# A tuned attention and feed-forward kernel on one core: 122 of some 1180 program steps put in another order

## The chip, the cores and the metric

The kernel runs on one core of a Trainium2 chip. The metric is the device time of one execution in microseconds (us); the runs shown give a median, a lowest and a highest value. A profile is one further execution, recorded by the hardware profiler: each engine's instructions with their start and duration. Engines: PE is TensorE (matmuls; PEld its weight loads), DVE is VectorE, ACT is ScalarE, POOL is GpSimd, SP is SyncE, which issues most of the transfers.

## The reference

Two blocks follow each other. The first is attention with a polynomial sketch instead of a softmax: each row of q and k (4 batches, 4 heads, 1088 rows, 32 columns) is turned into 64 features, products of two sketches of 8 values. The second is a feed-forward block with a product in place of an activation.

```python
def phi(x):
    a = np.einsum('rd,bhsd->bhsr', S1, x)
    b = np.einsum('rd,bhsd->bhsr', S2, x)
    return np.einsum('bhsi,bhsj->bhsij', a, b).reshape(*x.shape[:-1], r * r)
q_p, k_p = (phi(q), phi(k))
kv = np.einsum('bhsf,bhsd->bhfd', k_p, v)
z = np.sum(k_p, axis=2)
num = np.einsum('bhsf,bhfd->bhsd', q_p, kv)
den = np.einsum('bhsf,bhf->bhs', q_p, z)[..., None] + 1e-06
...
x = np.ascontiguousarray(attn_out.transpose(0, 2, 1, 3)).reshape(B * S, H * D)
a = x @ w1
b = x @ w2
h = a * b @ w3
return (h @ w_out)
```

x has 4352 rows of 128; w1 and w2 are 128 x 1024, w3 is 1024 x 1024 and w_out 1024 x 128.

## The kernel before

`make_steps` defines about 1180 small functions, the steps, each under a name such as `k0.gram0`, and each issues one or a few instructions. A long string, `ORDER`, names every step once. The kernel function takes the names in that order, runs each step, and then chains the instructions of every engine: an instruction of PE, DVE, ACT, POOL or SP may not be issued before the one that `ORDER` put ahead of it on the same engine. So `ORDER` alone decides what stands behind what on each engine; what one engine needs of another is waited for by semaphores. Two further tables go with it. `SLOTS` says, for each group of buffers, which buffer the first, second, third and so on allocation of the group takes. `POOL`, `ACTS` and `CPV` name the steps that run on another engine than the usual one. The large loads on SP are held back so that no more than `UNDER_WAY` of them are under way.

The steps that the prediction speaks of, with their lines before (the changed kernel has them one line up or three lines down):

- `warm0` to `warm11` (L255): fillers, matmuls of zeros that no one reads; the list `WARM` says how many each step issues (27, 2, 3, 4, 4, 4, 1, 2, 1, 1, 2, 2).
- `s.T`, `s.P` (L341, L391 to L393), `s.R` (L355): small matmuls on the sketch matrices S1 and S2; `s.c` (L369) copies the result of `s.R`, `s.blk` and `s.blkh` (L360, L365) make the block matrices from it, `s.AR` (L382) a third one.
- For each batch b of k: `kb.gram0` to `kb.gram4` (L659), the Gram matrix of k in tiny matmuls of 32 columns; `kb.lead0`, `kb.rest0` (L214, L651) split k into a leading word and the rest for it; `kb.T0`, `kb.T1` (L883, L889 to L891) and `kb.N0`, `kb.N1` (L912) bring the Gram matrix into sketch form, with `kb.Ta` and `kb.Tb` on DVE (L898, L201, L204, and L904) between them; `kb.kv0` to `kb.kv3` (L769) multiply features and v, where `kb.kp0` (L677) makes the features.
- For q: `q0.A0` (L1038), `q0.C0` (L1030) make the sketches, `qn.pt0`, `qn.pt1` (L1228, L1246) transpose the features `ph`, `qn.pc0`, `qn.pc1` (L1234) copy them out of PSUM, and `q0.x0`, `q0.x1` (L1267), `q1.x` (L1297) multiply them with k's sums.
- Of the feed-forward block: `g0.0a` to `g0.7a` (L1799) and `g0.0b` to `g0.7b` (L1809) are products of 128 rows of w1 or w2 with 512 columns of x, each one matmul in the program and two in the trace; `w1.a0` and the like (L470) prepare the weights on POOL.

A matmul on 4-byte numbers is one instruction in the code and appears as two weight loads and two matmuls in the trace (a transpose as one of each).

```python
for name in ORDER.split():
    n = len(traced)
    steps.pop(name)()
    ...
for ins in traced[seen:]:
    if ins.engine in chained:
        if ins.engine in last:
            tc.add_manual_dep(ins, last[ins.engine].name, behind, reason="order")
        last[ins.engine] = ins
```

Of the kernel before, what the change touches and what calls it, by code (L numbers as in the profile page):

```python
# [76 lines left out]
k0.load1 s.words kr0.load k0.tr1 s.pair s.low s.lead s.sum k0.max0 k0.max1 warm1 q0.max k0.tr0 warm2 kr0.tr kr0.kT  # L77
warm3 s.rest w1.load s.T s.P s.tc warm4 q0.l2 k0.kT1 s.Pc s.R k0.g k0.lead0 s.c s.blk k0.rest0 q1.tr k0.gram0 s.blkh
k1.zero s.Pm warm5 q0.l1 q0.A0 warm6 kr0.ab k0.lead1 q0.rm q0.sma q0.sta warm7 k0.kT0 v0.load v0.loadr k1.load k0.ab1
q0.sha k0.rest1 q0.C0 k0.gram1 k0.gram2 k0.gram3 k0.gram4 k0.ab0 k0.abc1 q1.max q0.C0t q0.sla q1.l2 k1.loadr s.Pp  # L80
k0.Gm k0.Gt k0.Ga w1.c1 k0.Gb k0.abc0 k0.T0 q1.l1 warm8 kr0.abc k0.kp1 q0.sca w1.j1 k0.Ta k0.kp0 k0.Gc w1.c0 k1.tr0
kr1.load k2.zero k1.tr1 k1.kT1 kr0.kp warm9 k0.N0 warm10 k0.Na warm11 k0.T1 k0.kv0 k0.Tc k0.Tb k0.N1 k0.Nb k0.Nh q1.rm
q0.al k0.Nf q0.phi0 q0.phi1 q0.A1 q0.smy w1.m1 k1.max q0.sty q0.shy k0.kv3 k0.kv1 k0.kv2 q0.sly s.KS k0.kvr kr1.tr
k0.kvm w1.m0 kr1.kT q0.p01 q1.C0 q1.C1 q0.C1 k0.kzt k2.loadr q0.pt0 q0.C1t q0.scy q0.p2 k0.kz q0.pt1 k0.kvc kr1.ab
k0.kqt q0.p12 q0.dn q0.de q0.rc w1.j0 q0.pc0 q0.pc1 q0.x0 k1.kT0 q0.x1 q0.xs0 q0.xs1 q0.xt0 w1.a0 q1.A0 k2.load
w0.load k1.lead0 q0.xc0 q0.xc1 k0.kq w1.a1 k2.max q0.xt1 k1.ab q0.xT0 q0.xT1 g0.4a q1.load g0.5a q1.sm w0.m1 q1.st
q1.Ct g0.4c g0.4b q1.sh q1.sl k1.rest0 g0.7b w0.c1 g0.7a k1.abt w0.j1 k1.gram0 w0.c0 s.RC q1.scy k1.gram1 kh2.load
q1.sca q2.tr g0.5c q1.al q1.p01 q1.p2 k1.gram2 k1.gram3 kr1.abc k1.gram4 w6.load w0.m0 g0.6b w0.j0 g0.7c g0.7m k1.Gm
q1.p12 k1.Gc g0.0a w2.load w0.a1 q1.dn q1.de q1.rc q1.bs k1.Gt g0.3a k1.Ga k1.T0 k2.kT1 k1.Gb g0.3c q1.restT g0.2a
q1.phi k1.T1 q1.pt0 g0.4m w0.a0 q2.max q2.l2 g0.6a k1.Ta k2.lead0 k2.rest0 g0.1a g0.2c k1.Tc g0.5b q3.tr g0.5m k1.Tb  # L90
# [5 lines left out]
k1.kv1 k2.T0 k1.kvr q3.sl q2.p2 k2.T1 q2.p12 q2.dn q2.de g1.4a q2.rc k3.max g0.3b g0.0m g1.1b kh3.load g1.4c k2.Ta
g1.2b q3.sc g1.2c w5.c k2.Tc k1.kvc k1.kqt k1.kq g0.3m q3.p01 g1.6c g1.3a g1.5m g1.3b q2.bs q2.phi0 q2.pT0 g1.2m g1.3c
q2.x q2.load k2.N0 k2.Tb k3.lead0 w9.a1 k2.N1 g1.4b q3.al q3.p2 q3.p12 q2.xT0 g2.5a k3.kT1 g2.5c g2.6a q3.dn q3.de
k2.Na g1.3m g2.4a g2.3a w5.m g2.4b g2.6c k3.rest0 g1.0b k2.Nr q3.rc g1.1m g1.4m g1.6b k2.Nb g0.2b kr1.kp w6.j q4.tr
g2.4c g1.6m w7.load w7.c q3.bs q4.max q2.restT w6.m w5.j w2.j q4.l2 w3.load w9.a0 k3.gram0 k3.gram1 k3.gram2 q3.load  # L100
# [5 lines left out]
w4.m g3.6c q3.restT q6.tr g3.6b g3.6m q4.Ct q4.sm w10.load f0.m k2.kp0 f4.o g3.1b f0.o g3.1m qr.max q6.max k3.kp1
q4.st k2.kv0 w4.a1 k3.kp0 k2.kv3 k2.kv1 k2.kv2 k2.kvr q4.sh qr.l2 k3.kv0 k3.kv1 f3.t k2.kvc k3.kv3 k3.kv2 k3.Na w4.a0
qr.l1 qr.rm q4.sl q4.sc q4.al k3.kvr k3.kvc g3.4a q6.l2 g3.4c g3.4b q4.p01 k3.Nr g3.3b q6.l1 w8.c g3.5a k3.Nb g2.4o
g3.4m f1.t f3.m w10.c k3.kqt g3.5c w8.m g3.3m q4.p2 q6.rm k3.kq f1.m f1.o q6.A0 q6.C0 w10.j q6.C1 g3.1o f3.o w8.j
q4.p12 q6.At g3.2b w10.m q6.Ct q4.dn g3.7a q6.sm q6.st w8.a0 w10.a0 qr.A0 qr.C0 qr.C1 g3.0o g2.1o g3.7c w10.a1 g0.3o  # L110
# [1824 lines left out]
```

## Time and profile before

| what | value |
|---|---|
| median of 3 runs | 245.37 us (245.28 to 245.43) |
| the profiled execution's own span, first to last instruction | 244.1 us |
| PE busy | 236.2 us (97% of the span), 2724 matmuls |
| DVE busy | 206.7 us (85%) |
| POOL busy | 161.9 us (66%) |
| ACT busy | 123.5 us (51%) |
| DMA packets | 31935, 22.06 MB |
| mean granted clock of TensorE | 0.998 of full speed |

The span does not hold what lies around the program, so it is 1.27 us shorter than the median of the runs. A line of the page or of a view names the engine, the line of the code, the operation and the tiles (out<-in, with the shape). "Idle" or "wait" is time in which an engine ran nothing, and the name behind it is what it seems to have waited for; "issue" means that nothing in the profile explains it. A window gives, for each engine, the busy time and the number of instructions in a stretch, then the granted clock, the share of the DMA engines in use and the GB/s.

### The profile page before, as it was taken

To read this page: it belongs to the slowest core of one execution; us is meant where nothing else is said; L and a number is where in the kernel's file an instruction comes from. 1 tells how busy PE (TensorE), PEld (TensorE's weight loads), DVE (VectorE), ACT (ScalarE), POOL (GpSimd) and SP (SyncE) were. 2 spreads that over 40 slices of the span, in tenths; PEclk is the share of its full clock that TensorE was granted. 3 is DMA by queue.
4 is the path that set the end of the run, shared out by engine and by line. 5 is a ranking of instruction groups with operands and counts; after the bars stand their busy time and mean duration, and the time that the engine had idled before them with its cause. 6 is when DMAs were issued, how large, how long until landed. Compare 5 with 4: busy or idle time off the path is not lost.

```text
span 244.1 us, 6745 instructions
## 1 busy us (share of the span) xinstructions
PE 236.2 (97%) x2724; PEld 129.8 (53%) x2724; DVE 206.7 (85%) x421; ACT 123.5 (51%) x246; POOL 161.9 (66%) x203
## 2 busy tenths in 40 slices
PE   8998999899999999999999999999999999999994
PEld 5887454545545646766566444444443354463363
DVE  2876988999899998997899878498989789999792
ACT  3976957675666764593012914355651164730010
POOL 4576658344856998764583889929999425883670
PEclk9999999999999999999999999999999999999999
DMA  7959797078859897200000000360000000000054
GB/s 201 265 143 325 181 227 190 6 197 224 220 141 251 188 217 190 59 1 3 3 0 0 4 0 3 59 113 3 1 0 0 0 3 0 0 1 3 12 90 93
DMA packets 31935, 22.06 MB, mean 90 GB/s; under 512 B 21280, under 2 KB 26528, under 8 KB 31904
## 3 DMA queue, kind: packets, MB, share of 16 engines
q1 hardware_dynamic: 31360, 21.11, 35.1%
q8 instruction: 21, 0.34, 0.6%
q10 hardware_dynamic: 544, 0.52, 0.6%
q14 instruction: 10, 0.08, 0.1%
HBM read 19.40 MB, written 2.23 MB: 89 GB/s over the span
## 4 chain that ended last, share of the span: by engine, by line
PE 87%; DMA 5%; ACT 2%; POOL 2%; DVE 1%; issue 1%; POOLq 0%; SPq 0%
PE b_ps L1809 12%; PE ps_o L1835 12%; PE ps_X L1673 11%; PE a_ps L1799 11%; PE ps_o L1759 10%; PE ps_w3o L534 6%; PE ps_Y L1673 6%; PE ps_Z L1673 3%; PE ps_g L659 2%; PE ps_x L1527 2%; PE ps_ac L1374 2%; DMA qh<-in_q_dram 2%; DMA k<-in_k_dram 2%; PE ps_or L1824 2%; POOL ph L1208 1%; PE idle_ps L255 1%
## 5 line engine op out<-in xcount | busy, mean ns | idle before, releaser
L1673 PE MATMUL ps_X<-xd,wv 64*128 64x512 f32 x112 | 36.3, 593 | 0.0
L1799 PE MATMUL a_ps<-xT,w 128*128 128x512 f32 (+1 forms) x80 | 36.1, 562 | 0.0
L1809 PE MATMUL b_ps<-xT,w 128*128 128x512 f32 (+1 forms) x80 | 35.6, 555 | 0.0
L1804 ACT COPY ffa<-a_ps 128x512 f32<-128x512 f32 (+1 forms) x38 | 20.1, 540 | 29.2 <-PE a_ps L1799 26.7
L1707 POOL TENSOR_TENSOR hc<-hc 128x512 f32<-128x512 f32 x16 | 20.7, 1304 | 15.7 <-DVE hc L1685 15.5
L1835 PE MATMUL ps_o<-ab,w3o 128*128 128x512 f32 x64 | 29.6, 600 | 0.0
L1680 ACT COPY hc<-ps_X 128x512 f32<-128x512 f32 x38 | 21.3, 590 | 16.1 <-PE ps_X L1673 12.9
L1815 DVE TENSOR_TENSOR ab<-ffa,b_ps 128x512 f32<-128x512 f32 (+1 forms) x40 | 23.9, 623 | 4.9 <-PE b_ps L1809 4.1
L501 POOL TENSOR_TENSOR w3c<-w3c,cv_m 128x512 int32<-128x512 int32 x16 | 21.2, 1344 | 4.2 <-DVE w3c L495 4.1
L1673 PEld LDWEIGHTS ps_X<-xd,wv 64*128 64x128 f32 x112 | 14.9, 186 | 13.1 <-issue 10.9
L1799 PEld LDWEIGHTS a_ps<-xT,w 128*128 128x128 f32 x80 | 14.1, 189 | 13.9 <-issue 8.8
L1809 PEld LDWEIGHTS b_ps<-xT,w 128*128 128x128 f32 x80 | 14.4, 190 | 13.1 <-issue 8.1
L1673 PE MATMUL ps_Y<-xd,wv 64*128 64x512 f32 x48 | 19.7, 594 | 0.0
L1835 PEld LDWEIGHTS ps_o<-ab,w3o 128*128 128x128 f32 x64 | 11.6, 190 | 13.4 <-issue 13.0
L534 PEld LDWEIGHTS ps_w3o<-wo,w3T 128*128 128x128 f32 x128 | 15.3, 192 | 2.4 <-issue 2.4
L534 PE MATMUL ps_w3o<-wo,w3T 128*128 128x128 f32 x128 | 15.7, 276 | 0.0
L1759 PE MATMUL ps_o<-hc,w3o 128*64 128x512 f32 x32 | 15.1, 595 | 0.0
L1759 PE MATMUL ps_o<-tt,ws 128*64 128x512 f32 x32 | 13.7, 594 | 0.0
L1680 ACT COPY hc<-ps_Y 128x512 f32<-128x512 f32 x14 | 8.1, 592 | 9.7 <-PE ps_Y L1673 6.6
L263 ACT ACTIVATE cv_c<-raw 128x1024 f32<-128x1024 f32 (+1 forms) x13 | 13.0, 1014 | 0.0
L1540 ACT COPY xd<-ps_x 64x256 f32<-64x256 f32 x24 | 8.8, 367 | 7.2 <-PE ps_o L1835 6.8
L1497 POOL COPY nz<-nz 32x8 f32<-32x8 f32 x32 | 11.1, 347 | 1.4
...
## 6 DMA issues: line engine op xcount, KB each, us to landing
...
```

The lines of the kernel that those rows point to most:

```text
L263: act.activation(dst, hi.bitcast(F32), ACT.Prelu, scale=2.0 ** -112, alpha=-2.0 ** 32)
L501: pool.tensor_tensor(d, d, x["m"][:, i * 512:(i + 1) * 512], ALU.add)
L534: pe.matmul(t["o"], w3T[ko][:, c], wo[:, c], start=c == 0, stop=c == NC - 1)
L1673: pe.matmul(x[bank], stat(j, u)[:, i * 128:(i + 1) * 128], rows(j, u), start=new, stop=True, tile_position=(u * 64, 0), skip_group_check=True)
L1680: cp(n(y))(x[k], x[bank])
L1707: on(f"h{g}.{i}m{k}").tensor_mul(both[0][k], both[0][k], both[1][k])
L1759: pe.matmul(acc_o[bank][half[0]:half[1]], w(i), x(i), start=n == 1, stop=n == (2 if j == 3 else 4), tile_position=(0, half[0]), skip_group ...
L1799: pe.matmul(x["a"][:, :w], w_of(0, c), xT[g][:, c0:c0 + w], start=True, stop=True)
L1804: cp(f"g{g}.{c}{su}c")(x["s"][:, :w], x["a"][:, :w])
L1809: pe.matmul(x["b"][:, :w], w_of(1, c), xT[g][:, c0:c0 + w], start=True, stop=True)
L1815: dve.tensor_mul(ab_sb[g, c][:, c0:c0 + w], x["s"][:, :w], x["b"][:, :w])
L1835: pe.matmul(o_ps[g], w3o[:, c], ab_sb[g, c], start=n == 1, stop=n == NC)
```

## The change

Of the names in `ORDER`, those from the 30th to the 345th stand in another order; 122 steps are moved against the rest. The loads on SP keep their order among themselves, and behind the 345th name nothing differs. The buffer tables are rewritten so that the allocations, which come in the new order, find free buffers. One step, `s.AR`, goes from DVE to POOL. Two steps are written so that they cope with an allocation made the other way round; they issue what they issued. The fillers' counts are the same.

```diff
-    qr.p12 qr.p2 s.KS s.Pp s.blk s.blkh s.low s.rest
+    qr.p12 qr.p2 s.AR s.KS s.Pp s.blk s.blkh s.low s.rest
...
-    "012345670214657210671306537457462512346127340273014526045721472352140327540542370673245716"
+    "012345707415625627067130635744265123416273402703154260475124572312140327540564237037425716"
...
-q1.pc0 q1.pt1 g0.1b w9.load k1.N0 s.AR q2.l1 q2.rm v3.zero q1.pc1 k1.N1 q1.x g0.6c g0.1c k1.Na k1.Nr k3.zero k2.gram0
+g0.5b q3.tr q1.pt1 g0.5m g0.1b w9.load q2.l1 s.AR g0.6a g0.1c q1.pc1 q1.x g0.6c k2.gram0 q2.rm k1.Na v3.zero k2.gram1
...
         @step(f"k{b}.T0")
         def _():
-            a["T"], a["Tr"] = two([D, H, r], "ps_T")
+            a["T"], rest = two([D, H, r], "ps_T")
+            if rest is not None:
+                a["Tr"] = rest
```

Three places are shown in the order of an engine's instructions. The first is on PE, at the start of the program, from kr's transpose (`ps_krt`) over S's words (`ps_st`, `ps_p`) to the first Gram step (`ps_g`) and `s.R` (`ps_s`); L255 and L254 are fillers. Before:

```order
L819 MATMUL ps_krt<-ident,kr_161 128x128
L255 LDWEIGHTS zeros
L255 MATMUL idle_ps<-zeros 128x256
...
L341 MATMUL ps_st<-ident,sk_x 32x8 x4
L391 MATMUL ps_p<-sk_x 32x32
L392 MATMUL ps_p<-sk_x 32x32
L393 MATMUL ps_p<-sk_x 32x32
...
L355 MATMUL ps_s<-sk_t,four 128x32
L659 MATMUL ps_g<-kk 32x64
L659 MATMUL ps_g<-k,kk 32x32
```

and in the changed kernel:

```order
L818 MATMUL ps_krt<-ident,kr_161 128x128
L254 LDWEIGHTS zeros
L254 MATMUL idle_ps<-zeros 128x256
...
L390 MATMUL ps_p<-sk_x 32x32
L391 MATMUL ps_p<-sk_x 32x32
L392 MATMUL ps_p<-sk_x 32x32
L340 MATMUL ps_st<-ident,sk_x 32x8 x4
L658 MATMUL ps_g<-kk 32x64
L658 MATMUL ps_g<-k,kk 32x32
...
L354 MATMUL ps_s<-sk_t,four 128x32
```

Between kr's transpose and S's words there were 4 fillers and are 2; between these and `s.R` there were 4 fillers and none is left. The Gram step stood behind `s.R` and stands ahead of it; 8 fillers come behind `s.R` now.

The second place is on PE too, from `k1.T1` (`ps_T`) over `q1.pt0` and `q1.pt1` (`ps_ph`), products of the feed-forward block (`a_ps`, `b_ps`) and `k1.N0`, `k1.N1` (`ps_N`) to `q1.x` (`ps_x`). Before:

```order
L891 MATMUL ps_T<-RS,G_b 32x32
L1246 MATMUL ps_ph<-ident,ph 128x128 x4
L1799 MATMUL a_ps<-xT,w_81 128x512 x2
L1809 MATMUL b_ps<-xT,w_81 128x512
L1246 MATMUL ps_ph<-ident,ph 128x128 x4
L1809 MATMUL b_ps<-xT,w_81 128x512
L912 MATMUL ps_N<-T_p,P2a 32x8 x4
L912 MATMUL ps_N<-T_p,P2b 32x8 x4
L912 MATMUL ps_N<-T_p,P2s 32x8 x8
L1297 MATMUL ps_x<-pT,kz_605 64x512 x2
```

and in the changed kernel:

```order
L254 MATMUL idle_ps<-zeros 128x256
L1249 MATMUL ps_ph<-ident,ph 128x128 x4
L1802 MATMUL a_ps<-xT,w_81 128x512
L913 MATMUL ps_N<-T_p,P2a 32x8 x4
L913 MATMUL ps_N<-T_p,P2b 32x8 x4
L913 MATMUL ps_N<-T_p,P2s 32x8 x8
L1812 MATMUL b_ps<-xT,w_81 128x512
L1249 MATMUL ps_ph<-ident,ph 128x128 x4
L1812 MATMUL b_ps<-xT,w_81 128x512
L1802 MATMUL a_ps<-xT,w_81 128x512
L1300 MATMUL ps_x<-pT,kz_597 64x512 x2
```

Ahead of `k1.N0` only one of the four feed-forward products and the first `ps_ph` are left; the other three products and the second `ps_ph` stand between `k1.N1` and `q1.x`. The filler `warm7` stands ahead of `q1.pt0` now.

The third place is on ACT: the copies of k's transpose (`kT`), of q's features (`pT`) and the step behind them (`xs`). Before:

```order
L794 COPY kz_605<-ps_kz 128x128
L799 COPY kvc<-ps_kv 128x256
L1234 COPY pT<-ps_ph 128x2x256 x2
L690 COPY kT<-ps_kt 128x512
L1280 COPY xs<-s_rc 128x256 x2
```

and in the changed kernel:

```order
L793 COPY kz_597<-ps_kz 128x128
L798 COPY kvc<-ps_kv 128x256
L689 COPY kT<-ps_kt 128x512
L1237 COPY pT<-ps_ph 128x2x256 x2
L1283 COPY xs<-s_rc 128x256 x2
```

`kT` stood behind `pT` and stands ahead of it.

More of the change, by code (lines that the diff above doesn't have):

```diff
@@ L76 @@
 c.zeros warm0 q0.load c.ident s.four c.act c.mask s.zero k0.zero v0.zero s.load k0.load0 k0.loadr q0.restT q0.tr
[L77 to L90, printed above, removed]
@@ L96 @@
[L96 to L100, printed above, removed]
@@ L106 @@
[L106 to L110, printed above, removed]
@@ L141 @@
-gr.4c gr.1b gr.0b g6.oT gr.6a h6.k8 g5.st h6.k9 g7.oT gr.7o1 gr.6b gr.6c gr.0m gr.0o1 gr.4m gr.4o1 gr.0o0 gr.4o0 gr.5m
-gr.5o0 g6.oS g6.st g7.oS g7.st gr.6m gr.6o1 gr.1m gr.6o0 gr.1o0 gr.5o1 gr.oT0 gr.1o1 gr.oT1 gr.st1
+k0.load1 s.words kr0.load k0.tr1 s.pair s.low s.lead s.sum k0.max0 k0.max1 warm1 q0.max k0.tr0 warm2 kr0.tr q0.l2
+kr0.kT w1.load warm10 s.rest k0.kT1 s.P s.T s.tc s.Pc q0.l1 k0.g k0.lead0 k0.rest0 k0.gram0 s.R warm9 warm3 q1.tr s.c
+s.blkh s.blk s.Pm warm4 q0.A0 warm5 kr0.ab warm6 k0.lead1 q0.rm q0.sma v0.load k1.zero q0.sta v0.loadr k1.load k0.kT0
@@ new lines @@
+k0.rest1 k0.ab1 k0.gram1 k0.gram2 q0.C0 k0.gram3 q0.sha k0.gram4 k0.ab0 s.Pp q1.max k0.abc1 q0.C0t k1.loadr q1.l2
+k0.Gm k0.Gt w1.c1 k0.Ga k0.abc0 q0.sla q1.l1 k0.Gb k0.T0 warm8 k0.kp1 k0.Ta q0.sca w1.j1 k0.Gc k0.kp0 kr0.abc w1.c0
+k1.tr0 kr1.load k1.tr1 k1.kT1 k2.zero kr0.kp k0.N0 k0.Na k0.T1 k0.kv0 warm11 k0.Tc k1.max k0.Tb k0.N1 k0.Nh q0.al
+k0.Nb q1.rm q0.phi0 k0.Nf kr1.tr q0.A1 q0.smy q0.phi1 q0.sty q0.shy w1.m1 k0.kv3 k0.kv1 k0.kv2 s.KS k0.kvr q0.sly
+q0.p01 q1.C0 w1.m0 kr1.kT q1.C1 q0.C1 k0.kvm k0.kzt q0.pt0 k0.kz q0.C1t q0.scy k0.kvc k2.loadr q0.p2 q0.pt1 k0.kqt
@@ new lines @@
+kr1.ab q0.p12 q0.dn w1.j0 q0.de q0.rc k1.kT0 q0.pc0 q0.pc1 q0.x0 q0.x1 k2.load q0.xs0 q0.xs1 q0.xt0 w1.a0 q1.A0
+w0.load k1.lead0 q0.xc0 q0.xc1 w1.a1 q1.load k0.kq k2.max q0.xt1 k1.ab q1.Ct q0.xT0 q0.xT1 w0.m1 g0.5a q1.sm g0.4a
+q1.st g0.4b w0.c1 q1.sh k1.rest0 q1.sl g0.4c s.RC k1.abt w0.c0 g0.7a w0.j1 g0.7b k1.gram0 k1.gram1 q1.scy q1.sca
+kh2.load q1.p01 g0.5c q2.tr q1.al k1.gram2 q1.p2 k1.gram3 g0.7c kr1.abc k1.gram4 w0.j0 w0.m0 w6.load g0.7m g0.6b k1.Gm
+k1.Gc q1.p12 w0.a1 g0.0a w2.load q1.dn q1.de q1.rc q1.restT q1.bs k1.Gt g0.3a k1.Ga k2.kT1 g0.3c g0.2a k1.Gb k1.T0
@@ new lines @@
+q1.phi k1.T1 g0.4m q2.max warm7 q1.pt0 q2.l2 w0.a0 k1.Ta g0.2c k1.Tc k2.lead0 q1.pc0 g0.1a k1.Tb k1.N0 k2.rest0 k1.N1
+g0.5b q3.tr q1.pt1 g0.5m g0.1b w9.load q2.l1 s.AR g0.6a g0.1c q1.pc1 q1.x g0.6c k2.gram0 q2.rm k1.Na v3.zero k2.gram1
+k3.zero k2.gram2 g0.1m k2.gram3 q3.max k1.Nr g0.0c k2.gram4 k2.kT0 q1.xT q3.l2 w9.c k1.Nb k2.ab q2.A0 q3.l1 q2.C0
+q2.C1 k1.kp0 v1.zero k2.abt g1.5a g1.5c g1.1a q2.Ct g1.7a k0.Nr q2.At g0.6m q3.rm q2.sm k2.Gm k1.kp1 g1.0a v1.loadr
+q2.st q3.A0 q3.C0 g1.1c k2.Gt w9.j q2.sh q3.C1 g1.2a q3.Ct g1.5b w2.m k3.load g1.7b v1.load q3.At w2.c q2.sl k2.Ga
@@ new lines @@
+g1.6a g0.0b k3.loadr g1.7c k1.kv0 w6.c k2.Gb q3.sm w5.load q2.sc q2.p01 q2.al g1.0c k2.Gc q3.st g1.7m k1.kv2 k1.kv3
+q3.sh w9.m k1.kv1 k2.T0 k1.kvr q3.sl q2.p2 k2.T1 q2.p12 q2.dn q2.de g1.4a q2.rc k3.max g0.3b g0.0m g1.1b kh3.load
+g1.4c k2.Ta g1.2b q3.sc g1.2c w5.c k2.Tc k1.kvc k1.kqt k1.kq g0.3m q3.p01 g1.6c g1.3a g1.5m g1.3b q2.bs q2.phi0 q2.pT0
+g1.2m g1.3c q2.x q2.load k2.N0 k2.Tb k3.lead0 w9.a1 k2.N1 g1.4b q3.al q3.p2 q3.p12 q2.xT0 g2.5a k3.kT1 g2.5c g2.6a
+q3.dn q3.de k2.Na g1.3m g2.4a g2.3a w5.m g2.4b g2.6c k3.rest0 g1.0b k2.Nr q3.rc g1.1m g1.4m g1.6b k2.Nb g0.2b kr1.kp
@@ new lines @@
+g3.6a k3.Tb v2.loadr k3.ab f4.t k3.Tc k3.abt w4.j g3.3c w3.a1 q4.A0 q4.C0 q4.C1 q4.At k3.N0 k3.N1 v2.load w3.a0 f0.t
+k2.kp1 f4.m w4.m g3.6c q3.restT q6.tr g3.6b g3.6m q4.Ct q4.sm w10.load f0.m k2.kp0 f4.o g3.1b f0.o g3.1m qr.max q6.max
+k3.kp1 q4.st k2.kv0 w4.a1 k3.kp0 k2.kv3 k2.kv1 k2.kv2 k2.kvr q4.sh qr.l2 k3.kv0 k3.kv1 f3.t k2.kvc k3.kv3 k3.kv2 k3.Na
+w4.a0 qr.l1 qr.rm q4.sl q4.sc q4.al k3.kvr k3.kvc g3.4a q6.l2 g3.4c g3.4b q4.p01 k3.Nr g3.3b q6.l1 w8.c g3.5a k3.Nb
+g2.4o g3.4m f1.t f3.m w10.c k3.kqt g3.5c w8.m g3.3m q4.p2 q6.rm k3.kq f1.m f1.o q6.A0 q6.C0 w10.j q6.C1 g3.1o f3.o
@@ new lines @@
+h4.0b4 h4.0a4 h6.s2 h4.1bh h4.2b1 h4.0ai h4.1a7 h4.0af h4.1b7 h4.2a1 h4.1a2 h4.0m21 h4.0T1 h4.2b2 h4.1ag h4.1bg h4.1a4
+h4.1b3 h4.2bc h4.1af h4.1b4 h4.2ac h4.2a6 h4.1ah h4.0m12 h4.1m11 h4.2a2 h4.2b6 h4.1bf h4.0T3 h4.1ai h4.2ae h4.2bh
+h4.1m21 h4.2be h4.3a1 h4.3b1 g0.st h4.1m12 h4.2ah h4.3bc h4.2b5 h4.3ac h4.3a2 h4.2b7 h4.2a7 h4.1m22 h4.3b2 h4.0T2
+h4.2bd h4.2m11 h4.2a5 h4.2ad h4.2b3 h4.3a6 h4.3ah h4.3ae h4.3b6 h4.3a5 h4.1T1 h4.3bh h6.1b1 h4.3ad h4.2bf h4.2a3
+h4.2bg h4.3m11 h4.2ag h4.3b5 h4.2m22 h4.2af h4.3a7 h4.3ag h4.2b4 h4.2a4 h4.3a3 h4.3be h4.3b7 h6.1bc h4.3bd h4.3b3
@@ new lines @@
+h6.0a1 h4.2ai h4.3a4 h4.3bg h6.1b6 h6.1a1 h4.2m21 h4.3bf h4.3b4 h6.0ac h6.0a6 h6.0b1 h4.3P1 h4.3af h4.1P5 h4.2T1
+h4.1T2 h4.2m12 h4.1T4 h4.0P1 h4.2T2 h6.1ac h4.2P5 h4.0P5 h4.3m22 h4.1T3 h4.0T4 h4.0P6 h4.3ai h4.3m21 h4.1P4 h4.2T3
+h4.2P2 h4.0P4 h6.1be h4.1P1 h4.3T1 h4.1P7 h4.3T2 h4.1P6 h4.3T3 h4.1P2 h4.3P5 h4.2P7 q4.ns h4.2P6 h6.0ae h4.3m12 h4.3P6
+h4.3P7 h4.2P1 h4.0P7 h4.k1 h4.2T4 h4.3T4 h4.3P2 h6.s3 h4.k3 h6.0bc h4.2P4 h4.0P2 h4.3P4 h4.k2 h4.k4 h4.k5 h4.2P3
+h4.1P3 h4.0P3 h4.3P3 gr.1a gr.1c h6.0b6 h6.0a7 h6.0be h6.0a5 h4.k7 h4.k8 h4.k9 h6.0b5 h6.1b7 h6.1a6 h6.0b7 h6.0bd
@@ L143 @@
+h6.k3 g4.oS h6.k2 h6.k4 h6.0P3 gr.7o0 g4.st gr.0a gr.5b h6.k5 h6.k6 h6.3P3 h6.1P3 h6.k7 g5.oS q6.ns gr.4a gr.3o0 gr.4b
+gr.0c gr.4c gr.1b gr.0b g6.oT gr.6a h6.k8 g5.st h6.k9 g7.oT gr.7o1 gr.6b gr.6c gr.0m gr.0o1 gr.4m gr.4o1 gr.0o0 gr.4o0
+gr.5m gr.5o0 g6.oS g6.st g7.oS g7.st gr.6m gr.6o1 gr.1m gr.6o0 gr.1o0 gr.5o1 gr.oT0 gr.1o1 gr.oT1 gr.st1
 """
@@ L916, in _ @@
         def _():
-            a["N"], a["Nq"] = two([128, r], "ps_N")
+            a["N"], rest = two([128, r], "ps_N")
+            if rest is not None:
+                a["Nq"] = rest
             by_head(a["N"], P2a, 0, True, True)
```

71 lines of the change are left out of this document (28 added, 43 removed).

## The prediction

> **What bounds the kernel now.** I read the page first, then the busy windows, then what PE waited for, and last the chain and the timeline around the three longest of those waits.
>
> ```profile
> span 244.1 us, 6745 instructions
> PE 236.2 (97%) x2724; PEld 129.8 (53%) x2724; DVE 206.7 (85%) x421; ACT 123.5 (51%) x246; POOL 161.9 (66%) x203
> q8 instruction: 21, 0.34, 0.6%
> ```
>
> PE is busy for 97% of the span. The third line is the queue that brings PE's own program: 21 transfers, 0.34 MB, so 16 KB each. The windows (busy us and count of each engine, then granted clock) say where the missing 3% lies:
>
> ```profile
> 40.00:50.00 10.00, 8.84 (x280) 5.24 (x279) 8.91 (x23) 5.42 (x10) 5.47 (x7) 1.00 0.23 59
> 50.00:60.00 10.00, 10.00 (x170) 5.16 (x169) 9.47 (x32) 7.67 (x11) 3.44 (x7) 1.00 0.87 233
> 60.00:200.00 140.00, 140.00 (x1398) 73.15 (x1399) 122.03 (x224) 69.36 (x135) 102.66 (x95) 1.00 0.28 65
> ```
>
> From 50 to 200 us PE never idles. Whatever the new order saves before 50 us shifts all of that forward; whatever it saves after is worth nothing. PE's waits in the first 60 us (total, times, longest):
>
> ```profile
> PE ps_g L659 <- issue: 1.6, 2, 1.2
> PE idle_ps L255 <- DVE zeros L229: 1.0, 1, 1.0
> PE ps_kv L769 <- issue: 0.9, 1, 0.9
> PE ps_xs L1287 <- ACT xs L1280: 0.3, 1, 0.3
> PE ps_kt L685 <- DMA k<-in_k_dram: 0.3, 1, 0.3
> PE ps_ph L1246 <- POOL ph L1208: 0.2, 1, 0.2
> ```
>
> Without the 1.0 us before the first instruction, 3.3 us are left: that is the most this change can win. Of it 2.5 us are "issue", a wait on nothing that the profile shows. Windows cut at the three issue waits tell what it is:
>
> ```profile
> 0.00:13.87 13.87, 12.59 (x221) 10.28 (x221) 7.93 (x24) 9.14 (x23) 7.27 (x41) 1.00 0.85 239
> 13.87:19.60 5.73, 5.17 (x124) 4.26 (x125) 4.04 (x16) 4.26 (x11) 3.77 (x7) 1.00 0.53 160
> 19.60:46.00 26.40, 24.90 (x505) 14.51 (x505) 22.38 (x59) 19.50 (x42) 16.34 (x20) 1.00 0.74 195
> ```
>
> Between the first and the second wait PE took 249 matmuls and weight loads, between the second and the third 1010; with the semaphore instructions, which have no row here, that is one piece and four pieces of 256. So the waits fall where a new 16 KB piece of the program begins. The pieces between had time to come: 256 instructions of tiny matmuls last some 3 to 6 us, of long ones far more. Around the third wait (a row of the chain: start, us, what; a window; a row of the timeline; the program queue between 44.2 and 45.5 us):
>
> ```profile
> 43.26 1.01 PE ps_x L1297 x4
> 42.90:45.90 3.00, 2.92 (x158) 1.98 (x159) 2.93 (x8) 2.42 (x6) 0.67 (x4) 1.00 0.02 5
> 46.98 0.19 PE L659 MATMUL ps_g<-k,kk 128*32 128x32 f32 x1 [1.16 <-issue]
> q8 instruction: 1, 0.02, 5.5%
> ```
>
> The window from 42.90, where the L912 steps N0/N1 start, holds 317 matmuls and loads; the last 256 are the piece, which so begins 61 instructions in, among the last of L912's 64, near 43.1. They need 2.7 us, to 46.98 − 1.16 = 45.82. The next piece is asked for after 44.2 and can be run at 46.98, 3.9 us after that beginning.
>
> **The change part by part.** All compared times are PE's place in the profiled execution (244.1 us; the median of the runs is 1.27 us more, 245.37, and I keep that distance). PE runs the same matmuls, in another order up to some 60 us and in the same order behind.
>
> *Start to the first issue wait.* The first Gram step moves ahead of S's step (L355) and nearly all fillers, right behind the S words:
>
> ```profile
> 8.66 0.69 DVE L651 TENSOR_TENSOR kk<-k,kk 128x512 f32<-128x512 f32 x1
> 7.71 0.43 PE idle_ps L255 x4
> 8.33 0.17 PE ps_p L391 x2
> 9.18 0.35 PE ps_s L355 x2
> 9.52 0.57 PE ps_g L659 x22
> 10.47 0.26 PE L1038 MATMUL ps_a<-Rh,q 128*128 128x32 bf16 x4
> ```
>
> It needs DVE's kk, which ends at 9.35, so it still starts at about 9.5. PE has 2 fillers of 0.11 us (0.43/4) and the S words (from 7.71 + 0.43 to 8.33 + 0.17: 0.36 us) ahead of it, is done at 7.71 + 0.58 = 8.3 and idles 1.2 us. Then come the Gram step (0.57 at most), L355 (0.35), and 1 + 3 + 4 fillers (0.87), which hide what ACT and POOL make of L355's result: q0.A0 (L1038) starts at 9.5 + 1.79 = 11.3 at the latest, or 0.8 later than before. Behind it stand 5 fillers where 3 stood (+0.2), so PE arrives at the first issue wait's place 0.8 to 1.0 us later than at 13.86; I take 14.7. The piece could be run at 14.27; if it comes no later, its wait of 0.41 is gone. **Term A: 14.7 − 14.27 = +0.4**; if the piece comes as much later as PE enters the one before (some 0.7 to 1.0), up to +1.0.
>
> *To the second issue wait.* Fillers that stood here have moved forward, and kv0 (L769) waits for its kp on DVE without them:
>
> ```profile
> 16.63 1.21 DVE L677 TENSOR_TENSOR kp<-kab 128x1024 f32<-128x1024 f32 x1
> 18.25 0.26 PE ps_kv L769 x14
> 20.35 0.47 PE L769 MATMUL ps_kv<-kp,v 128*32 128x64 f32 x18 [0.91 <-issue]
> ```
>
> kp ended at 17.84; with the 0.7 us by which this stretch begins later passed on to DVE it ends near 18.5. From kv0 to the issue wait PE took 19.44 − 18.25 = 1.2 us, and now has 2 fillers and kr1's transpose more (0.5): it arrives near 20.2, and of the wait of 0.91 some 0.25 is left, as the piece was usable at 20.35 and the one before is entered 0.4 later, of which I count a quarter. **Term B: 20.45, which is +0.1 in all, or −0.3 after A.** Its bounds are 20.2, where the work alone would bring PE, and 20.65.
>
> *20.4 to 38 us.* kr1's transpose (0.26) leaves for the stretch before. On ACT the kT copy goes ahead of the pT copies:
>
> ```profile
> 24.83 0.61 ACT L690 COPY kT<-ps_kt 128x512 f32<-128x512 f32 x1
> 24.59 1.08 PE L1267 MATMUL ps_xt<-pT,kz 128*64 128x256 f32 x8
> ```
>
> So L1267 starts 0.61 later than its own work allows, about 24.8 (+0.2). The xs copy behind it no longer stands behind kT, so the 0.3 wait stays about as it is; the first FFN product then waits for POOL's w as before (+0.2), T0 and T1 stand together (−0.2), and the filler warm7 fills what was the 0.24 wait for ph. Net 0, between −0.4 and +0.4: **term C1: −0.1**, which puts PE at its old place, 38.3.
>
> *38 to 44 us, the heart of it.* Four long steps (g0.5b, pt1, g0.1b, g0.6a) move from before N0/N1 to behind them, and N0 needs DVE's T_p:
>
> ```profile
> 38.16 0.18 DVE L898 TENSOR_REDUCE T_g<-ps_T 32x4 f32<-32x32 f32 x1 [0.34 <-PE ps_T L891]
> 38.59 0.99 DVE L204 SCALAR_TENSOR_TENSOR T_p<-T_g,T_t 32x32 f32<-32x32 f32 x1
> 39.51 0.86 DVE L214 TENSOR_SCALAR kk<-k,k_g 128x1152 f32<-128x1152 f32 x1
> 16.52 0.18 DVE L204 SCALAR_TENSOR_TENSOR T_p<-T_g,T_t 32x32 f32<-32x32 f32 x1
> 38.27 1.27 POOL L470 TENSOR_TENSOR w<-w,cv_m 128x512 int32<-128x512 int32 x1
> 39.02 1.72 PE a_ps L1799 x4
> ```
>
> From 38.16 DVE does T_g, T_t, T_p, the 0.86 us kk and then the last T_p operation: to 40.37 + 0.2 = 40.55. PE has only pt0 (to 39.02, where the products begin) and one product (half of 1.72, 0.86) and is there at 39.9: a wait of some 0.7 that was not there before. T_p took 0.99 us here and 0.18 for the batch before; here it ended at 39.58, as POOL's L470 did (39.54). By these bounds the wait is 0 to 0.75. In both orders L470 follows ph on POOL; if ph is done some tenths earlier, as C1 supposes, so is L470. I take T_p at 0.8, nearer its own row. **Term C2: +0.55.** [...]
>
> *The third issue wait.* The same 256 instructions are now entered behind 0.86 us products instead of behind tiny L912 matmuls. The piece begins inside q1.x (L1297), and PE's sequencer takes instructions ahead of their execution:
>
> ```profile
> 0.00:110.50 110.50, 106.17 (x1854) 66.03 (x1855) 94.51 (x225) 75.37 (x145) 72.24 (x105) 1.00 0.68 178
> 109.00:110.50 1.50, 1.50 (x16) 1.50 (x15) 1.34 (x3) 1.47 (x2) 0.08 (x1) 1.00 0.00 0
> q8 instruction: 14, 0.23, 0.9%
> ```
>
> The last line is the program queue up to 110.4 us: 14 pieces. A request follows the entry of the piece before, and the first piece asked for began at the first wait, so at instruction 442, some 450 with the semaphores. The 15th request, at 110.5, belongs to the entry of instruction 450 + 13·256 = 3778; but by then 3709 matmuls and loads had started, some 3750 with semaphores. Among long products PE's sequencer is thus some 30 instructions ahead, 1.5 us by the second row. Ahead of q1.x now stand g0.6a and g0.1b (0.86 us each), so I take it to be 1.4 us ahead: the piece comes 3.9 − 1.4 = 2.5 us after q1.x starts, and PE needs 45.82 − 43.26 = 2.56 us to get there. **Term D: −1.16**, with 0 as its other end.
>
> [...]
>
> *s.AR* moves from DVE (0.82 us) to POOL:
>
> ```profile
> 42.34 0.82 DVE L382 TENSOR_TENSOR AR<-Sc,mask2n 128x64 bf16<-128x64 f32 x1
> ```
>
> POOL has no row for it; POOL is busy 5.47 of the 10 us there (window above), so even twice 0.82 us has room, and PE waits for neither: 0. If POOL's k2 kk were pushed by it, k2's Gram would have 1 us or more of cover in q1.x. Transfers, loads and their order are as before: 0. After 50 us nothing moves but PE's place: 0.
>
> Sum: +0.4 − 0.3 − 0.1 + 0.55 − 1.16 = **−0.6 us**: a profiled execution of 243.5 and a time of 244.8.
>
> **The rivals.**
>
> 1. *The third issue wait stays* (slower). It decides if the request goes by the execution of q1.x, not by the sequencer running ahead, or if the wait belongs to the Gram step and not to the piece. For it: at 43.1 the request did come about 1.1 us behind the execution. Against it: the request at 110.5. Then D is about 0 (3.9 against 2.56 us: a wait of 1.3) and the sum is +0.7: 246.0. If the early pieces go by execution too (A +1.0), it is +1.4: 246.8.
> 2. *N0 does not wait*, as T_p ends early: C2 is 0 and the time 244.2.
> 3. *The new uncovered waits eat it all.* The Gram step, kv0, L1267 and N0 each wait for an engine with nothing under them; 0.6 us more than I count (C1 at +0.4, C2 at 0.74) gives 245.4.
> 4. *The clock drops.* PE idles 1.2 us from 8.3 on, with fewer fillers around; were the clock halved over the next 3 us of work (an assumption: no window after the start shows a drop), that would cost 1.5 us more: 246.3. Against it: after the idle 1.16 at 46 us the granted clock of its window is still 1.00. [...]
>
> **How the numbers follow.** Forecast 0.5, rival 1 0.17, rival 2 0.13, rival 3 0.15, rival 4 0.05. The measurement tells 0.2%, 0.5 us, from no change: faster is under 244.88, slower over 245.86. The forecast's own spread (C1 and T_p, 244.3 to 245.3) puts a little over half of it under 244.88; with rival 2 that is 0.42 faster. Its rest and rival 3 make 0.36 the same; rivals 1 and 4 make 0.22 slower. The range runs from rival 2's 244.2 to 246.4, which leaves out the far part of rival 1 and what is worse than rival 4.
>
> **What would show it.** In the changed kernel's waits of PE: no issue wait in k2's Gram step (D right; one of 1 us or more: rival 1); an issue wait at L768 of 0.1 to 0.5 (B); a wait of about 1.2 for DVE's kk near 9.5 (A); a wait of 0 to 0.74 at L913 for T_p on DVE (C2); the first FFN product at 27.4 to 27.8 (C1). PE must again be busy without a break from 50 to 200 us; a new idle time there would make the whole sum wrong, and so would a granted clock under 1.00 in the windows up to 20 us.

## The result, and the profile after

The changed kernel is slower: 248.23 us in the median of six runs (247.21 to 249.89) against 245.43 (245.28 to 245.66), a ratio of 1.0117 with a 95% interval of 1.0094 to 1.0141. The forecast was 244.8, its range 244.2 to 246.4. The profiled execution took 247.65 us. Medians and ratios leave out the executions that lay more than 1.5% above the fastest of their kernel. The page of the changed kernel (the span and the engines' busy time):

```profile
span 245.9 us, 6744 instructions
PE 237.2 (96%) x2724; PEld 130.7 (53%) x2724; DVE 206.0 (84%) x420; ACT 123.1 (50%) x246; POOL 161.0 (65%) x204
```

The span grew by 1.8 us, from 244.1; the matmuls are as many as before. In every execution on record that has both figures, the time is 1.74 to 1.86 us above its own span. So the profiled execution of the kernel before took some 245.9 us, half a microsecond over the median of 245.4, and the distance of 1.27 us that the prediction kept compares two different executions; with 1.8 the forecast span of 243.5 would have been a time of 245.3.

The windows of the changed kernel (busy us and count of each engine, granted clock, DMA share, GB/s) say where:

```profile
40.00:50.00 10.00, 8.49 (x243) 4.66 (x249) 6.97 (x16) 5.64 (x11) 4.08 (x8) 1.00 0.40 102
50.00:60.00 10.00, 10.00 (x154) 4.54 (x130) 9.02 (x31) 7.57 (x11) 3.56 (x4) 1.00 0.62 183
60.00:200.00 140.00, 140.00 (x1471) 73.77 (x1472) 122.52 (x226) 68.04 (x133) 104.09 (x96) 1.00 0.29 69
```

From 50 to 200 us PE is never idle, as before; the loss lies ahead of that. The window from 40 to 50 us, the heart of the change, now holds 1.51 us of idle time where it held 1.16. PE's longest waits in the first 60 us of the changed kernel (total, times, longest):

```profile
PE ps_g L658 <- issue: 1.9, 2, 1.5
PE idle_ps L254 <- DVE zeros L228: 1.0, 1, 1.0
PE ps_kv L768 <- DVE kp L676: 0.6, 1, 0.6
PE a_ps L1802 <- POOL w L469: 0.5, 1, 0.5
PE ps_g L658 <- DVE kk L650: 0.4, 1, 0.4
```

The third issue wait, in k2's Gram step, is the 1.5 of the first row. The chain of the changed kernel (start, us, what) at the three places:

```profile
15.04 0.38 issue
15.42 0.58 PE ps_g L658 x20
...
39.87 1.12 PE a_ps L1802 x2
40.99 0.36 PE ps_N L913 x32
...
44.56 1.01 PE ps_x L1300 x4
45.57 1.60 PE ps_g L658 x78
47.18 1.51 issue
48.69 0.48 PE ps_g L658 x12
```

PE passes the first issue wait at 15.42 (before 14.27), starts q1.x at 44.56 (43.26) and comes out of the third wait at 48.69 (46.98). So +1.15 us comes from the start, +0.15 from the stretch between, and +0.41 from q1.x to the end of the third wait, where −1.16 was forecast.

### The profile page after: what moved, and what is told of

Its sections match the earlier page's. It is cut to its first block, busy times and chain, and to the rows that moved or that the text cites. A ratio compares the mean times of both kernels' runs of the same rounds, so it can differ in the third digit from the quotient of the medians.

```text
span 245.9 us, 6744 instructions
## 1 busy us (share of the span) xinstructions
PE 237.2 (96%) x2724; PEld 130.7 (53%) x2724; DVE 206.0 (84%) x420; ACT 123.1 (50%) x246; POOL 161.0 (65%) x204
## 4 chain that ended last, share of the span: by engine, by line
PE 93%; DVE 2%; issue 2%; POOL 1%; ACT 1%; POOLq 0%
PE b_ps L1812 13%; PE a_ps L1802 13%; PE ps_o L1838 12%; PE ps_X L1676 11%; PE ps_o L1762 10%; PE ps_w3o L533 6%; PE ps_Y L1676 6%; PE ps_g L658 3%; PE idle_ps L254 3%; PE ps_Z L1676 3%; PE ps_x L1530 2%; PE ps_ac L1377 2%; PE ps_or L1827 2%; PE ps_kv L768 2%; PE ps_ab L701 1%
## 5 line engine op out<-in xcount | busy, mean ns | idle before, releaser
L1812 PE MATMUL b_ps<-xT,w 128*128 128x512 f32 (+1 forms) x80 | 36.1, 557 | 0.0
L1683 ACT COPY hc<-ps_X 128x512 f32<-128x512 f32 x38 | 21.3, 590 | 16.1 <-PE ps_X L1676 12.9
L1838 PEld LDWEIGHTS ps_o<-ab,w3o 128*128 128x128 f32 x64 | 11.6, 190 | 13.4 <-issue 13.0
L533 PEld LDWEIGHTS ps_w3o<-wo,w3T 128*128 128x128 f32 x128 | 15.3, 192 | 2.4 <-issue 2.4
L262 ACT ACTIVATE cv_c<-raw 128x1024 f32<-128x1024 f32 (+1 forms) x13 | 13.1, 1018 | 0.0
```

The source lines that it names most:

```text
L262: act.activation(dst, hi.bitcast(F32), ACT.Prelu, scale=2.0 ** -112, alpha=-2.0 ** 32)
L533: pe.matmul(t["o"], w3T[ko][:, c], wo[:, c], start=c == 0, stop=c == NC - 1)
L1683: cp(n(y))(x[k], x[bank])
L1812: pe.matmul(x["b"][:, :w], w_of(1, c), xT[g][:, c0:c0 + w], start=True, stop=True)
L1838: pe.matmul(o_ps[g], w3o[:, c], ab_sb[g, c], start=n == 1, stop=n == NC)
```

## The experiments

All ratios are to the kernel before, run on the same chip in the same session. "The third wait" is the issue wait in k2's Gram step.

### The change again, and its halves

Up to the 245th name the two orders hold the same names, so the halves can be exchanged. Written as slices of the two orders:

```diff
 e1_again:       ORDER = CHANGE
-ORDER = CHANGE
+e2_first_half:  ORDER = CHANGE[:245] + BEFORE[245:]
+e3_second_half: ORDER = BEFORE[:245] + CHANGE[245:]
```

> The changed kernel once more. Theory 1 (a program piece can be run a fixed time after PE executes the first instruction of the piece before, so the moved work brings nothing): the same place of the time lost, 248.2 us, an issue wait of over 1 us in k2's Gram step (L658) again, about 3.9 to 4.2 us after PE enters the piece before. Theory 2 (the clock: the early part has more idle time on PE, and the granted clock rises late or drops again): the filler matmuls of the start show when the clock rises; over 6 us after the start again if it belongs to the change, anywhere between 4 and 7.6 us if it is chance; the runs differ among themselves by 2 us or more.

> The change up to the 245th name only (start, fillers, k0, q0), the order of before behind it. If the first half carries the loss: 246.3 to 248, PE enters the first FFN product 0.8 us or more later than before, and the runs scatter. If the loss is the second half's: 245.2 to 245.6. Theory 2 alone: the scatter of the changed kernel (over 1.5 us between its runs) is here and not in the second half.

> The order of before up to the 245th name, the change behind it: N0 and N1 ahead of three long products, s.AR on POOL. Theory 1: the third issue wait stays at 1.0 to 1.6 us, as PE's sequencer enters the piece only with q1.x; 245.3 to 246.3. If the sequencer ran ahead among long products, as predicted: the wait is under 0.3 us and the time 244.2 to 244.9.

The change again: 247.27 us (before 245.46), 1.0100 (1.0064 to 1.0136). The first half: 247.43, 1.0078 (1.0059 to 1.0097). The second half: 245.42, 1.0008 (0.9974 to 1.0042). So the loss sits with the first half, and the second half alone neither loses nor gains in the median, though its profile has a third wait of 1.5 us. Two of six runs of the change, two of six of the first half and one of twelve of the second had a mean granted clock of 0.992 or 0.993, which none of the 17 runs of before had (of 81 later ones two had 0.992 or less).

The profile of the change again (246.93 us) is the cleanest one to hold against the sum. Its chain:

```profile
43.87 1.01 PE ps_x L1300 x4
...
46.48 1.50 issue
```

Here everything up to q1.x cost what was forecast: it begins 0.61 us later than before (43.26), and A, B, C1 and C2 make +0.55. Then comes a third wait of 1.50 where none was forecast.

### Long products moved behind the piece's beginning

```diff
-... q1.pc0 q1.pt1 g0.1b w9.load ... k2.gram1 k2.gram2 ...
+... q1.pc0 q1.pt1 w9.load ... k2.gram1 g0.5b g0.1b k2.gram2 g0.5m g0.1m ...
```

> The kernel before with two long products, g0.5b and g0.1b (1.7 us on PE), taken from ahead of N0 and put between k2's second and third Gram step, so that the piece that was too short, 2.7 us of work, holds 4.4 us. Theory 1: the issue wait of 1.16 us is gone or under 0.2, the time 244.2 to 244.6. If the wait belongs to the Gram step and not to the piece's length: it stays at about 1.2 and the time at 245.2 to 245.7.

247.40 us, 1.0084 (1.0058 to 1.0110), not the 244.2 to 244.6 that were expected. PE's three longest waits in this kernel, without the one ahead of its first instruction:

```profile
PE a_ps L1802 <- DVE kabt L744: 1.5, 1, 1.5
PE ps_ab L726 <- DVE RC L939: 0.7, 1, 0.7
PE ps_g L658 <- issue: 0.6, 1, 0.6
```

The 0.6 is the first issue wait; the third is gone. Its place is taken by waits for DVE, 2.2 us in all, which the two products had covered. That the third wait belongs to a piece of 256 short instructions which PE runs through in less time than the next one takes to come (2.7 us against 3.9 in the kernel before) is thus right; the price was paid elsewhere.

### What holds the request: another PSUM buffer

In the change, as in the kernel before, k2's first Gram step takes the PSUM buffer of the product g0.6a, so PE waits there for ACT's copy of it (g0.6c). The change put g0.6a right ahead of q1.x, so this copy comes late. ACT's row of the copy, and the program queue from 46.3 to 47.5 us, both of the changed kernel:

```profile
44.60 0.59 ACT L1807 COPY ffa<-a_ps 128x512 f32<-128x512 f32 x1 [1.13 <-DVE N_t L200]
q8 instruction: 1, 0.02, 5.4%
```

The copy ends at 45.19. From 44.5 to 46.3 the program queue moved nothing; the piece was asked for only behind 46.3 (a piece counts as asked for when the queue begins to move it). The three kernels below give this Gram step the buffer of g0.5b, which is free long before, and exchange the two buffers in all that follows. Nothing else differs; each character of the table is the buffer of one allocation.

```diff
-"012345707415625627067130635744265123416273402703154260475124572312140327540564237037425716"
+"012345707415625627067130635744265123416273402703154260475124572312740321540564231031425176"
...
```

> The changed kernel with the same order, but k2's first Gram step takes the PSUM buffer that the product g0.5b left (copied out some 2 us earlier) and not the one that ACT's copy of g0.6a frees; the two buffers change places in all that follows. Theory (PE's sequencer, held just behind the piece's beginning by the wait for that copy, asks for the next piece only then): the request comes up to 1.5 us earlier, the wait of 1.5 us in k2's Gram step falls to 0.4 or less, and the time is 1.1 to 1.3 us below the change's, about 246.0. Rival (the request goes by the execution of the matmuls in front, whatever the buffer): the wait stays at 1.4 to 1.6 and the time at the change's 247.3.

> Order of before up to the 245th name, that of the change behind it (as in e3_second_half, 245.4 us), with the same exchange of the two PSUM buffers. Theory: the third issue wait, 1.5 us there, falls to 0.4 or less, and the time to 244.1 to 244.4, below both kernels. Rival (request by execution): 245.4 and a wait of 1.5.

> The kernel before with the same exchange of buffers and nothing else. Here the copy of g0.6a ended at 43.14 us, close to where the piece begins in any case. Theory: the request comes 0.3 to 0.4 us earlier, the third issue wait is 0.8 instead of 1.2, the time 245.0 to 245.1. Rival: no difference, 245.4.

The second half without and with the exchange is the pair that shows it, as both run the same order. ACT's copy, the program queue from 45.2 to 46.3 us and the chain, without the exchange (e3_second_half):

```profile
43.62 0.59 ACT L1807 COPY ffa<-a_ps 128x512 f32<-128x512 f32 x1 [1.13 <-DVE N_t L200]
q8 instruction: 1, 0.02, 5.4%
43.58 1.01 PE ps_x L1300 x4
44.59 1.56 PE ps_g L658 x76
46.15 1.51 issue
```

and with it (f2_second_slot; the program queue here from 42.3 to 43.4 us):

```profile
44.06 0.59 ACT L1807 COPY ffa<-a_ps 128x512 f32<-128x512 f32 x1 [1.13 <-DVE N_t L200]
q8 instruction: 1, 0.02, 5.4%
44.02 1.01 PE ps_x L1300 x4
45.03 1.82 PE ps_g L658 x88
46.85 0.59 PE ps_ab L726 x16
```

Without the exchange the piece is asked for 1.0 to 2.1 us after the copy's end (44.21); with it, 0.6 to 1.7 us ahead of q1.x's start, and the third wait falls from 1.51 us to nothing. The copy itself ends later than it did (44.65). The four profiles at full clock that have the new second half without the exchange agree on the place of the request: the queue began to move the piece 1.1 to 1.4 us after the copy's end (46.4 against 45.19 in the change, 45.6 against 44.49 in the change again, 45.3 against 44.21 in e3_second_half, 45.9 against 44.56 in f4_change_under3). So the buffer decides it in these profiles. That PE's sequencer stops at the wait for the copy is the theory put on record ahead of these runs; no run shows it, and g3_second_again below does not fit it.

The changed kernel with the exchange also has no third wait, and takes 246.29 us, 1.0040 (1.0011 to 1.0069), where the change had 1.0117 and 1.0100. Near the 246.0 expected: by these ratios about 0.6 to 0.8% was lost by this wait. Its chain, and the program queue from 46.6 to 46.7 us (f1_change_slot):

```profile
46.54 1.01 PE ps_x L1300 x4
47.55 1.88 PE ps_g L658 x89
q8 instruction: 1, 0.02, 60.2%
```

Here the piece was asked for 0.1 us behind q1.x's start and came just in time; the forecast had it 1.4 us ahead. h1_change_fill below, the same order with 9 fillers (18 instructions) more in front, has it between 42.9 and 43.0, 1.8 us ahead of q1.x (44.75). So the place at which the piece begins likely counts too. What is left of the loss is the start, below.

Two expectations failed here. The second half with the exchange takes 245.37 us, 0.9998 (0.9976 to 1.0021), not 244.1 to 244.4; its twelve runs lie from 244.4 to 245.9, those of e3_second_half from 244.5 to 248.0. The exchange took away the longest times and left the median. And the kernel before with the exchange has a third wait of 1.6, 245.44 us, 0.9990 (0.9966 to 1.0014): in the kernel before, the copy ended at 42.55 + 0.59 = 43.14, as the piece began. With the exchange the piece was asked for between 43.9 and 44.0, 1.6 us behind q1.x's start (42.35), and before between 44.2 and 44.3, 1.0 us behind it (43.26). Why the request is late there is not shown; that the piece is entered among tiny matmuls, with no long product ahead of them, is a guess.

### The start

```diff
 f4_change_under3:   the change
-UNDER_WAY = 4
+UNDER_WAY = 3
```

> The changed kernel with at most 3 large loads of SP under way at a time instead of 4. It asks whether the first pieces of the program come late because the loads hold the queues. Theory (they do): the first issue wait falls by 0.3 to 0.7 us, PE passes it at 14.5 to 15.0, and the runs scatter less; the later loads may come late, which would show as PE waits for DMA, so the time lies between 246.5 and 248.5. Rival (they come late for another reason): PE passes the first issue wait where the change does, 14.7 to 15.4, and the time is 247.3 or more.

247.65 us, 1.0107 (1.0060 to 1.0153), and the runs scatter no less (246.86 to 250.38). PE came past the place of the first issue wait at 14.80, as the theory had it, but the change again did so too (14.72), so one profile tells nothing of it. The run showed something else. Its chain and a window (busy, then granted clock):

```profile
46.54 2.04 issue
49.18:52.59 3.41, 3.41 (x90) 1.78 (x75) 1.83 (x8) 0.00 (x0) 2.28 (x3) 0.50 0.24 38
```

A third wait of 2.04 us, and 0.6 us behind it 3.41 us at half clock. The profile of f1_change_slot has the same behind its first issue wait (chain, window, and the program queue from 14.0 to 15.4 us):

```profile
14.66 1.99 issue
17.53:20.94 3.41, 3.41 (x18) 2.99 (x17) 2.43 (x9) 1.75 (x5) 1.40 (x3) 0.50 0.46 111
q8 instruction: 1, 0.02, 5.7%
```

So in this run the first piece was asked for behind 14.0 us and PE passed the wait at 16.65, 2.4 us later than before; in the change again it was asked for at 11.6 to 12.9. Between, the loads come in two waves: in f1_change_slot the DMA share was 1.02 from 10.0 to 11.5, 0.65 from 11.5 to 12.5 and 1.04 from 12.5 to 14.0. By the prediction's count PE enters the piece before some 0.7 to 1.0 us later than in the old order, and the request could miss the gap. Two kernels test it:

```diff
 g1_start_back_slot: f1_change_slot with the names ahead of k0.gram3 in the order of before
-kr0.kT w1.load warm10 s.rest k0.kT1 s.P s.T s.tc s.Pc q0.l1 k0.g k0.lead0 k0.rest0 k0.gram0 s.R warm9 warm3 q1.tr s.c ...
+kr0.kT warm3 s.rest w1.load s.T s.P s.tc warm4 q0.l2 k0.kT1 s.Pc s.R k0.g k0.lead0 s.c s.blk k0.rest0 q1.tr k0.gram0 ...
 h1_change_fill: f1_change_slot with 9 fillers more, all ahead of k0.gram0
-WARM = [27, 2, 3, 4, 4, 4, 1, 2, 1, 1, 2, 2]
+WARM = [27, 2, 3, 4, 4, 4, 1, 2, 1, 1, 11, 2]
-... w1.load warm10 s.rest k0.kT1 s.P s.T s.tc ...
+... w1.load s.rest k0.kT1 s.P s.T warm10 s.tc ...
```

> The changed kernel with the exchanged buffer (as f1_change_slot), and with the steps ahead of k0.gram3 put back into the order that they have before the change; warm9 and warm10 go back to k0.N0. Theory (what is left of the loss after the exchange is the start: the first issue wait passed at 14.7 to 16.7 us instead of 14.1 to 14.5, sometimes with a dropped clock behind it): PE passes the first issue wait at 14.1 to 14.5, no run shows a mean clock of 0.993, and the time falls from 246.3 to 245.4 or less. Rival (the loss lies between the first issue wait and 38 us): the time stays at 246.0 to 246.5.

> The kernel of g1_start_back_slot once more, for a profile at full clock (that run's profile had a granted clock of 0.66). Theory: the first issue wait over at 14.1 to 14.5 us, no issue wait over 0.3 in k2's Gram step, a span of 243.0 to 244.0. Rival: a wait of 1 us or more in k2's Gram step.

> The changed kernel with the exchanged buffer (f1_change_slot, 246.3 us) and 9 fillers more, all ahead of the first Gram step in the stretch in which PE waits for kk: 18 instructions, so that the piece which PE enters at 10.8 to 11.1 us begins 18 instructions earlier in the program, at about 10.2, where the order of before entered it (10.0). Nothing else moves. Theory (the start loses time because the piece is entered later and its request then falls, in some runs, into the second wave of bulk loads): the first issue wait is over at 14.1 to 14.6, no run has a mean clock of 0.993, and the time is 245.0 to 245.6. Rival (the order itself makes the start late, by what q0.A0 and the steps behind it wait for): 246.0 to 246.5 as f1_change_slot, with the 0.993 runs.

With the start put back the time is 245.07 us, 0.9985 (0.9963 to 1.0008): all that was left of the loss is gone, 0.55%, some 1.3 us. The profile of this kernel (h2, 245.25 us, span 243.5) has a first issue wait of 0.6 and no row for a third, and PE passes the first at 14.38.

With the fillers alone the time is 245.71, 1.0021 (0.9998 to 1.0043), halfway. The runs above 246.5 us are one of eleven, where f1_change_slot had six of twelve, and none has a clock of 0.993 (four of twelve there had 0.993 or less). The chain of h1_change_fill:

```profile
8.83 1.31 PE idle_ps L254 x11
10.14 0.52 PE ps_g L658 x28
10.66 0.33 PE ps_s L354 x2
10.99 1.09 PE idle_ps L254 x9
...
15.31 0.70 PE ps_g L658 x32
```

No issue wait is left at 15.3 (it was to end at 14.1 to 14.6), and PE does not wait for kk. What is left is work: the Gram step, S's step and nine fillers stand ahead of q0.A0, and the fillers in front ran 0.8 us past the end of kk (9.36), so that the Gram step began at 10.14. So the late tail went with the fillers, which move the place of the piece, and some tenths belong to the order; the interval still touches that of f1_change_slot, so the split between the two is likely, not shown. That the request queues behind the second wave of loads was not tried by itself, and not every profile fits it: in this one the piece was asked for between 13.0 and 13.1, with a DMA share of 1.07 from 13.0 to 13.5. What holds the first request stays open.

### Covering the third wait with wanted work

The kernel before with one product, which it runs some 4 us later in any case, laid ahead of k2.gram3:

```diff
-g0.1m k2.gram1 k2.gram2 q3.max k2.gram3 g0.0c k2.kT0 k1.Nb q1.xT k2.gram4 q3.l2 k2.ab ... k2.abt g1.5a g1.5c g1.1a
+g0.1m k2.gram1 q1.xT k2.gram2 g1.5a q3.max k2.gram3 g0.0c k2.kT0 k1.Nb k2.gram4 g1.5c q3.l2 k2.ab ... k2.abt g1.1a
```

> The kernel before with one feed-forward product, g1.5a, moved ahead of k2.gram3 (its copy and q1.xT with it). It lays 0.86 us of work that is wanted anyway into the stretch in which the program's piece is awaited. Theory: the third issue wait falls from 1.2 to 1.6 us to 0.3 to 0.8, nothing new is waited for, and the time is 244.4 to 244.8. Rival (the product had covered the wait for k2's ab or kabt behind it): a new wait of up to 0.9 us at the next product, and the time 245.2 to 245.5.

> The kernel of g2_product_forward once more (244.93 against 245.43, 0.9979, 0.9954 to 1.0004). Theory: again 0.1 to 0.3% below before, its third issue wait 0.5 or less. Rival: no difference from before.

244.93 us, 0.9979 (0.9954 to 1.0004), and once more 244.54, 0.9973 (0.9953 to 0.9994): faster than the kernel before by about a quarter of a per cent, though the first interval still holds 1. Span and waits of the second profile:

```profile
span 242.6 us, 6748 instructions
PE ps_xs L1290 <- ACT xs L1283: 0.3, 1, 0.3
PE ps_g L658 <- issue: 0.3, 1, 0.3
PE ps_ph L1249 <- POOL ph L1211: 0.2, 1, 0.2
```

The 0.3 is the first issue wait. The third has no row, and no new wait came in its place: unlike in e4_two_products, the product is taken from behind, so no cover is lost in front.

### The second half once more

> The kernel of e3_second_half once more, on the chip of the two others. Its twelve times lay in two groups, 244.5 to 245.5 and 246.6 to 248.0. Theory (the request for the third piece is held by ACT's copy in every run): the profile shows a third issue wait of 1.4 to 1.7 again, and the median lies 0.5 to 1.0 above f2_second_slot's, 245.9 to 246.4. Rival (held in some runs only, as the copy's time varies): a profile of a run near 244.6 shows the wait at 0.5 or less, and the median stays at 245.4.

245.35 us, 1.0007 (0.9976 to 1.0037). The median speaks for the rival: the piece is not late in every run of this kernel. So does its profile, taken at a granted clock of 0.85: the piece was asked for between 43.8 and 43.9, 2.1 us ahead of q1.x (46.01) and before ACT's copy of g0.6a had begun (46.05), and no third wait has a row. So the wait for that copy does not hold the request each time, and what decides it is not shown. How large the third wait is in the runs that have no profile, and why taking it away is worth 0.6 to 0.8% under the new start and nothing in the median under the old one, stays open.

## Why the prediction was wrong, point by point

- **What bounds the kernel**: right. PE is busy without a break from 50 to 200 us in these profiles (in e4_two_products 9.73 of the first 10 us, as the wait for kabt ends there), and whatever is lost ahead of that is lost for good.
- **Term D, −1.16, is the step that failed.** The prediction put the request 1.4 us ahead of q1.x's execution since it counted PE's sequencer some 30 instructions ahead among long products, an estimate from the request at 110.5. In f2_second_slot the request did come that early (1.6 us ahead), but the change itself put a semaphore wait right behind the piece's beginning: k2's Gram step waits for ACT's copy of g0.6a, which the change had moved to directly ahead of q1.x. The request came some 1.8 us behind q1.x's start (46.4 against 44.56), and the wait became 1.51 us instead of 0. With the other buffer it is 0: in f2_second_slot as the forecast had it, the request 1.6 us ahead of q1.x, in f1_change_slot with a request 0.1 us behind it and so by a margin of almost nothing. That the buffer makes the difference is shown at full clock; how it holds the request is not. The prediction listed T_p, kk and w as what PE would wait for, and didn't ask when the buffer that the Gram step writes comes free. Rival 1 (246.0, or 246.8 with A at 1.0) had the outcome for this wait right, for a different reason, and its times were too low as well. The program queue moves such pieces one by one (21 of 16 KB in the profile of before, for 2724 matmuls and as many weight loads). Under the new order the third wait was 0 with the one buffer (f1, f2) and 1.50 to 2.04 us with the other (after, e1, e3, f4).
- **Term A, +0.4, bound 1.0**: in the change again the added work came as counted, but the term took the piece to come no later than before, and in three other profiles (the change, e2, f1) PE waited for it. It measured +0.45 in the change again, +1.15 in the first profile and +2.4 in f1_change_slot (16.65 against 14.27), so the term scatters and the bound was too low. Putting the start back is worth 0.55%.
- **Term B, −0.3**: the second issue wait is gone from both profiles of the change, but the 0.6 wait for DVE's kp stands there instead; DVE's kp reached PE late, as supposed. The 0.91 us that the term was to cut was particular to that one profile: six other profiles with the old order up to there (e3, e4, f2, f3, g2, h3) have 0.36, none, 0.63, 0.08, 0.09 and 0.09.
- **Term C1, −0.1**: right as far as it shows; from the first issue wait to q1.x both profiles of the change lost 0.15 us, which is what B, C1 and C2 make together.
- **Term C2, +0.55**: the size was right, the place wrong. N0 did not wait for T_p; the product ahead of it waited 0.5 for POOL's w, until 39.87, and T_p's last operation ended at 40.74, before N0 began at 40.92. Rows of the changed kernel:

```profile
39.10 0.76 DVE L203 SCALAR_TENSOR_TENSOR T_p<-T_g,T_t 32x32 f32<-32x32 f32 x1
40.57 0.17 DVE L905 TENSOR_TENSOR T_p<-ps_T,T_p 32x32 f32<-32x32 f32 x1
38.54 1.27 POOL L469 TENSOR_TENSOR w<-w,cv_m 128x512 int32<-128x512 int32 x1
```

  The 0.76 us operation on T_p again ends with POOL's L469 (39.86 and 39.81), as that of 0.99 us did in the kernel before (39.58 and 39.54); why the two end together is not shown.
- **s.AR, 0**: right; no wait of PE names it.
- **Rival 4, the clock**: it dropped, in one of the first six runs of the change and in two of the next six, but no profile shows it behind the 1.2 us idle that the rival named. In all three profiles that have it (first half, f1, f4), 3.41 us at half clock follow an issue wait of 1.98 to 2.04 us, and cost up to 1.7 us (half of them, an estimate). The waits for k and for kk (0.4 to 1.0 us) brought none. The 3 us at half clock that the rival counted with were an assumption; the kernel before shows the like at its start, where 15 fillers took 3.2 us from 1.0 us on and the next 12 took 1.3 us, and measured behind an idle stretch are these 3.41 us.

Put together for the first profile: −0.6 forecast, +1.57 for D (+0.41 against −1.16) and +0.75 for A give +1.7; the span grew by 1.8. The median moved by 2.8. Of the rest, some 0.45 is the profiled execution of before, which lay that far over its median, and 0.6 the profiled execution of the change, which lay under its own (247.65 against 248.23).
